# Two attention-and-FFN schedules: the first four tiles' q and k in blocks of four heads, bias products as units of their own, twelve output buffers

## The chip, the cores and the metric

The kernel runs on one core of a Trainium2 chip. The metric is the device time of one execution in microseconds (us). The engines are PE (TensorE, matrix products), DVE (VectorE), ACT (ScalarE), POOL (GpSimd) and SP (SyncE, which here only issues transfers). PE writes its results into PSUM, which has eight banks of 128 x 512 fp32.

## The reference

Attention over q, k, v of shape [4, 8, 768, 64] (batch, heads, positions, head size). A query sees the 95 positions before it and itself, and the first 8 positions of its sequence (the global keys). A linear bias with one slope for each head (ALiBi) is taken off the scores. The result is read as 3072 rows of 512 numbers and goes through a layer with three weights and a maximum:

```python
scores = scale * np.matmul(q, k.transpose(0, 1, 3, 2))
keep = is_global | is_local
dist = np.where(is_global & ~is_local, float(n_local), np.abs(rel))
scores = np.where(keep, scores - slopes * dist, -1e9)
x = softmax(scores) @ v                      # -> [3072, 512]
h = np.maximum(np.maximum(x @ w1, x @ w2), x @ w3)   # w1..w3 [512, 768]
out = h @ w_out                              # w_out [768, 512]
```

(The last lines are the reference put together and shortened.)

## The kernel before

The 3072 rows are cut into 24 tiles T of 128 rows, six for each sequence of the batch. Two tiles form a pair G for loading. The FFN works on seven chunks of 4, 2, 2, 4, 4, 4 and 4 tiles.

All work is written out by hand in one string, SCHEDULE (lines 24 to 86). It is a list of units such as `F0.4.1@3`: a letter for the kind, numbers for what it works on, behind them for most copying units a digit for the engine (0 ACT, 1 DVE, 2 POOL), and behind the @ the buffer. The loop of lines 545 to 552 emits the units in that order; each engine executes its own units in the order of the string, and the framework adds the waits between engines that data and buffers need. SP issues transfers in the same manner, in the order of the string.

The kinds that matter here:

- `l` loads q, k or v (L213 for the first four tiles together, called group 12; L220 else), `c` casts them to bf16 (L185), `v` casts v into the value tile (L238).
- q and k have to be transposed. For the first pairs PE does it: `x` (L252, L258), and `y` copies the result from PSUM into a tile qkT (L266 for the first four tiles, L269). Later pairs use a transposing transfer `X` (L274).
- `G` puts the first 8 keys of a sequence into qkT (L289, L291), `V` puts their values into a value tile (L299 on POOL, L301 on ACT and DVE). `V` of a tile writes over rows that the attention of that same tile still reads, so it follows that tile's `A`.
- `S` are the scores of a tile and a group of four heads. S1.0, for instance, is tile 1, heads 0 to 3. With a last digit of 1, two matmuls first put the bias into PSUM (L313), and the score matmuls add to it (L321); with 0 there are only score matmuls, and the bias is applied after the exponential as a multiplication by a table, `m` (L337 for two blocks, L339 for the first tile of a sequence). `e` is the exponential on ACT (L328).
- `A` multiplies by the values (L363, L366), `n` normalises on DVE (L374, L375). The result is transposed for the FFN by PE (`t`, L390, and the copy `u`, L393) or by a transposing transfer `Z` (L396).
- `F` is one of the three products for one of six blocks of 128 hidden columns: `Fc.f.j@bank`, four matmuls (L405). `f` takes it out of PSUM: j = 0 copies (L419), j = 1 and 2 take the maximum on DVE (L421, L424).
- `O` is the product with w_out for one tile (L429), `o` copies it to an output buffer (L444), `s` stores it (L450). `E` does the last chunk (L453 to L479).
- `w`, `W`, `q`, `Q` load and cast weights. `D` are dummy matmuls (L506); `B` and `K` make the tables of the bias, `R` their common part.

`F`, `O`, `x` and `t` take one of the eight PSUM banks, `S` and `A` two neighbouring ones, named behind the @. A unit that takes a bank waits until the unit that last read the bank is done; so the choice of banks in the string decides which copy a matmul waits for.

Before the change, the tile qkT of the first four tiles has the layout [128, 2 tiles, q or k, 4 head pairs, 128]; a copy `y` of one half of the heads writes four separate pieces of it. Output buffers are six: three in the buffers of the small weight loads (wst0) and three in those of the large ones (wst1).

Of the kernel before, what the change touches and what calls it, by code (L numbers as in the profile page):

```python
# [12 lines left out]
FP32 = mybir.dt.float32  # L13
# [26 lines left out]
    l2.4.2@1 x3.1.2@7 Q1.2 l1.5.2@3 F0.5.2@0 c1.4.2.2@0 F1.0.2@1 v7.1.2 f1.4.1.1 y3.1.2.0 G6.0 c0.4.2.2  # L40
    f1.2.0.0@2 f0.5.2.1 f1.0.2.1@1 F1.2.1@5 f1.2.1.1 Q0.2 S6.0.0@2 e6.0@4 l0.5.2@4 S7.0.0@6 S7.1.0@0
    S6.1.0@4 F0.4.2@2 f0.4.2.1 e7.1@5 F1.5.0@3 F1.1.0@0 m7.1.1 e7.0@6 m7.0.1 F1.3.0@1 F1.5.1@2 x4.1.2@6
    f1.5.0.0@1 F1.2.2@3 m6.0.1 f1.2.2.1 v8.1.2 l1.6.2@5 e6.1@7 m6.1.1 x4.0.2@7 f1.5.1.1 f1.1.0.0@3 F1.1.1@0
    f1.1.1.1 f1.3.0.0@4 y4.1.2.0@0 A7@4 V7.0.2 v9.0.2 G7.0 v9.1.2 F1.3.1@1 n7@0 y4.0.2.0 Q2.0 c1.5.2.0@2
# [5 lines left out]
    V9.1.1 m10.0.1 S10.1.0@0 e10.1@6 V9.0.0 G10.1 O1.1@7 F2.5.1@2 f2.5.1.1 t8@3 F2.4.1@0 O0.0@1 m10.1.1 X11  # L50
    S11.1.0@4 l1.7.2@0 f2.4.0.0@4 o1.1.0@2 e11.1@4 v11.0.0 u8.1@0 S11.0.0@2 v10.0.1 f2.4.1.1 A10@6 V10.0.2
    e11.0@7 V10.1.0 X12@2 o0.0.1@2 n10@0 F2.5.2@0 F2.0.2@1 X13 l2.8.2@0 F2.1.0@4 F2.1.2@5 F2.1.1@2 F2.0.1@3
    m11.1.1 f2.5.2.1@0 Z9 F2.4.2@0 Z10 m11.0.1 f2.1.0.0@1 f2.1.1.1 l2.6.2@1 f2.4.2.1 A11@6 n11@3 O1.0@2
    o1.0.0@1 t11@0 u11.0 F2.3.2@4 l0.7.2@1 f2.1.2.1 f2.0.1.1 f2.0.2.1 f2.3.2.1 F2.2.2@3 l0.8.2@2 v12.0.2
# [531 lines left out]
```

## Time and profile before

| what | us |
|---|---|
| median of three runs (176.34 to 176.47) | 176.45 |
| the profiled execution's own time | 176.6 |
| its span, first to last instruction | 174.7 |
| PE busy | 166.9 |
| DVE busy | 127.7 |
| ACT busy | 102.4 |
| POOL busy | 48.9 |

The span is what the profile shows from the first to the last instruction; 1.9 us of the execution lie around it. A row of the timeline reads: start, duration, engine, line of the kernel, operation, what is written and from what, how many instructions, and in brackets how long the engine had been idle before and what released it. PEld is the weight load of PE, which overlaps the matmuls; its idle time alone doesn't mean that PE stood. In the chain of waits each row is a start, a length and what it consists of.

### The profile page before, as it was taken

The numbers are of one execution on the slowest core, as the hardware profiler recorded it, in microseconds if no ns is written. First come the engines' busy times: TensorE is split into PE (matmuls) and PEld (weight loads), VectorE is DVE, ScalarE is ACT, GpSimd is POOL, SyncE is SP. The second block draws the span as 40 slices with busy tenths as digits, with TensorE's granted clock in tenths as the row PEclk, the third lists the DMA queues.
The fourth block names the chain that finished last, engine by engine and source line by source line (L and its number), as shares of the span: only waits on it lengthen the run. The fifth ranks groups of instructions, "written<-read, shape, count | busy, mean of one in ns | idle before, by whom it ended". The sixth has DMA issues, their size and how long they took to land.

```text
span 174.7 us, 3862 instructions
## 1 busy us (share of the span) xinstructions
PE 166.9 (96%) x1489; PEld 93.5 (54%) x1510; DVE 127.7 (73%) x259; ACT 102.4 (59%) x153; POOL 48.9 (28%) x94
## 2 busy tenths in 40 slices
PE   7799999999999999999999999999999999999992
PEld 2346745576956867644456445554444554444442
DVE  7798969784868988589697287839859993059930
ACT  5979895487995876746257994721375651310022
POOL 4056536349370300196614003200203210000000
PEclk9999999999999999999999999999999999999999
DMA  5999999999999898998989498999992134047106
GB/s 148 352 292 312 363 351 379 294 319 345 270 230 267 193 145 194 290 319 198 232 146 196 119 253 200 290 159 260 272 184 68 32 90 64 0 180 240 60 10 234
DMA packets 66658, 37.35 MB, mean 214 GB/s; under 512 B 24144, under 2 KB 61904, under 8 KB 66640
## 3 DMA queue, kind: packets, MB, share of 16 engines
q1 hardware_dynamic: 66496, 37.04, 84.5%
q8 instruction: 12, 0.20, 0.5%
q10 hardware_dynamic: 144, 0.07, 0.1%
q14 instruction: 6, 0.05, 0.1%
HBM read 25.17 MB, written 6.29 MB: 180 GB/s over the span
## 4 chain that ended last, share of the span: by engine, by line
PE 83%; DVE 5%; DMA 4%; ACT 3%; issue 2%; SPq 1%; ACTq 0%
PE psum L405 50%; PE psum L429 18%; PE psum L321 5%; DMA rawqq<-in_q_dram 4%; PE psum L363 4%; PE psum L366 3%; PE psum L258 2%; DVE qkT L266 1%; ACT P L328 1%; PE psum L390 1%; DVE h L421 1%; DVE P L337 1%; PE psum L313 1%; SPq L213 1%; ACT qb L185 1%
## 5 line engine op out<-in xcount | busy, mean ns | idle before, releaser
L405 PE MATMUL psum<-xT,w 128*128 128x512 bf16 (+1 forms) x491 | 99.3, 348 | 1.1
L405 PEld LDWEIGHTS <-w 128*128 128x128 bf16 x504 | 47.5, 98 | 43.1 <-issue 2.7
L328 ACT ACTIVATE P<-psum 128x1024 bf16<-128x1024 f32 (+1 forms) x48 | 43.3, 953 | 13.5 <-PE psum L321 13.2
L421 DVE TENSOR_TENSOR h<-h,psum 128x512 bf16<-128x512 bf16 (+1 forms) x42 | 24.6, 604 | 16.1 <-PE psum L405 12.6
L429 PE MATMUL psum<-wo,ht 128*128 128x512 bf16 (+2 forms) x148 | 32.9, 362 | 0.6 <-issue 0.3
L337 DVE TENSOR_TENSOR P<-P,wmask 128x1024 bf16<-128x1024 bf16 x35 | 23.8, 695 | 6.2 <-ACT P L328 6.1
L424 DVE TENSOR_TENSOR ht<-h,psum 128x512 bf16<-128x512 bf16 (+1 forms) x42 | 26.1, 643 | 3.0 <-PE psum L405 2.4
L419 ACT CAST h<-psum 128x512 bf16<-128x512 f32 (+1 forms) x32 | 15.6, 517 | 20.1 <-PE psum L405 17.9
L429 PEld LDWEIGHTS <-ht 128*128 128x128 bf16 x156 | 14.0, 98 | 14.1
L238 POOL CAST va<-rawv 64x512 bf16<-64x512 f32 x26 | 16.5, 636 | 13.6 <-DMA rawv<-in_v_dram 12.8
L375 DVE TENSOR_TENSOR xb<-psum,rz 128x512 bf16<-128x512 f32 x24 | 16.6, 691 | 0.8
L299 POOL COPY va<-vaf 4x260 int32<-4x260 int32 x15 | 5.9, 395 | 37.5 <-PE psum L366 37.2
L321 PE MATMUL psum<-qkT 64*128 64x128 bf16 x352 | 14.9, 217 | 1.2 <-DVE qkT L266 0.9
L321 PEld LDWEIGHTS <-qkT 64*128 64x128 bf16 x352 | 10.3, 94 | 9.6 <-issue 6.8
L363 PEld LDWEIGHTS <-P 128*128 128x128 bf16 x192 | 12.3, 97 | 2.4
L363 PE MATMUL psum<-va,P 128*128 128x65 bf16 x160 | 12.5, 193 | 0.1
L444 ACT COPY ost<-psum 128x512 f32<-128x512 f32 x11 | 6.4, 589 | 8.9 <-PE psum L429 8.2
L366 PEld LDWEIGHTS <-P 128*128 128x128 bf16 x160 | 10.4, 97 | 1.5 <-issue 0.3
L434 ACT COPY ost<-psum 128x512 f32<-128x512 f32 (+2 forms) x5 | 2.3, 480 | 15.1 <-PE psum L429 15.0
L366 PE MATMUL psum<-va,P 128*128 128x65 bf16 x128 | 9.9, 193 | 0.0
L301 ACT COPY va<-vaf 4x520 bf16<-4x520 bf16 x10 | 6.2, 620 | 3.8 <-PE psum L366 3.7
L374 DVE RECIPROCAL rz<-psum 128x8 f32<-128x8 f32 x24 | 4.8, 202 | 4.7 <-PE psum L366 3.7
(69 smaller groups left out, 134.4 us busy)
## 6 DMA issues: line engine op xcount, KB each, us to landing
rawv<-in_v_dram SPq DMA_DIRECT2D x12, 512.0 KB, 6.3
rawq<-in_q_dram SPq DMA_DIRECT2D x10, 512.0 KB, 7.3
rawk<-in_k_dram SPq DMA_DIRECT2D x10, 512.0 KB, 7.0
out_dram<-ost SPq DMA_DIRECT2D x19, 256.0 KB, 2.6
wst<-in_moe_w_dram SPq DMA_DIRECT2D x3, 1024.0 KB, 10.9
wst<-in_moe_w_dram SPq DMA_DIRECT2D x3, 512.0 KB, 8.1
wost<-in_moe_w_out_dram SPq DMA_DIRECT2D x3, 512.0 KB, 7.3
out_dram<-ost SPq DMA_DIRECT2D x9, 128.0 KB, 1.8
```

What stands on the lines that cost most here:

```text
L238: copies[how](heads(va(T))[64 * e:64 * e + 64, :, 0:D], src)
L321: nc.tensor.matmul(sp[:, hh, j2, ds], qT(T - ds, 1)[hsl, jp], qT(T, 0)[hsl, jp], start=not how, stop=True, skip_group_check=True)
L328: nc.scalar.activation(P[:, :, 0:n], sps[T, g].rearrange("p a b d n -> p (a b) d n")[:, :, 0:n], AF.Exp, bias=0.0, scale=scale)
L337: mul(P, P, wmask[:, g, :, 0:2])
L363: nc.tensor.matmul(o, P[:, i, 0], heads(va(T))[:, h], start=True, stop=(t == 0), skip_group_check=True)
L366: nc.tensor.matmul(o, P[:, i, 1], heads(va(T - 1))[:, h], start=False, stop=True, skip_group_check=True)
L375: nc.vector.tensor_tensor(out=x.rearrange("p (g h) d -> p g h d", g=2), in0=o4[:, :, :, 0:64], in1=rz[:, :, :, None].to_broadcast([128, 2, ...
L405: nc.tensor.matmul(ps, w123[f // 2][:, j, dm, (f % 2) * 128:(f % 2) * 128 + 128], xT[c][:, dm], start=(dm == 0), stop=(dm == 3))
L419: copies[how](h01, ps)
L421: nc.vector.tensor_max(h01s[c, f], h01s[c, f], ps)
L424: nc.vector.tensor_max(dst, h01s[c, f].rearrange("p (t e i) -> p t e i", e=2, i=64), ps.rearrange("p (t e i) -> p t e i", e=2, i=64))
L429: nc.tensor.matmul(po, ht[c][:, f, tt * 128:(tt + 1) * 128], wo[:, f, cols], start=(f == 0), stop=(f == NF - 1))
```

## The change

1. The tile qkT of the first four tiles gets the layout [128, q or k, half of the heads, 2 tiles, 2 head pairs, 128]. One copy `y` now writes one block that lies together, and the scores of a group of heads read only its own block. `G` is adapted to it.
2. The two bias matmuls become a unit `b` of their own, which takes the banks; `S` with a last digit of 1 adds to them. There are eight such units. The scores S1.1 get the bias too, and the multiplication m1.1.1 is left out. Four dummy units are added, ten matmuls of 256 columns in all.
3. Output buffers are twelve, called os (a new entry of RINGS), laid over the place of wst1 in one tile that holds wst0 as well.
4. SCHEDULE has 781 units in place of 770. Many units move by a few places, get another bank, or another engine. Among the moves: v9, v16 and v17 go from POOL to ACT; u2 from ACT to DVE; u6 from DVE to ACT; v21.0 stands ahead of f4.1.0 on ACT; V4.0 ahead of f0.3.0; the store s0.1 ahead of Z15.

The diff, with the string cut to its first lines and to the places that are spoken of:

```diff
 SCHEDULE = """
...
-    y0.0.1.0@0 w0.2@2 D3.256@1 x12.1.1@1 y0.1.1.1 S0.1.1@2 c1.12.0.1 c0.12.0.1 S1.1.0@4 K1 x12.1.0@6
-    y0.1.0.1 G0.2 y1.0.1.0@1 e1.1@0 m1.1.1 v0.0.2 v1.0.2 e0.1@1 v0.1.2 D3.256@0 x12.0.0@0 y0.0.0.0 S1.0.1@2
-    w1.0@0 G1.0 e1.0@2 y1.1.0.1 S0.0.1@4 e0.0@3 y1.1.1.1 y1.0.0.1 S2.1.1@6 e2.1@4 v1.1.2 S2.0.1@2 G2.2
-    v2.1.1 v2.0.1 A0@0 n0@0 v3.0.2 l2.2.2@2 w1.1@1 A1@4 V1.1.2 e2.0@5 v3.1.2 n1@1 S3.0.1@6 c0.2.2.0@2 V1.0.1
+    x12.1.1@1 y0.0.1.0@0 K6 y0.1.1.1 b0.1@2 c1.12.0.1 b1.1@4 D3.256@6 S1.1.1 c0.12.0.1 S0.1.1 v0.0.2
+    x12.1.0@6 y0.1.0.1 G0.1 w0.0@1 w0.2@2 y1.0.1.0@1 e1.1@0 v0.1.2 D3.256@0 x12.0.0@0 v1.0.2 v1.1.2 e0.1@1
+    y0.0.0.0 b1.0@2 b0.0@4 D2.256@7 S1.0.1 G1.0 e1.0@2 S0.0.1 y1.1.0.1 y1.1.1.1 w1.0@0 b2.1@6 S2.1.1 e0.0@3
+    e2.1@4 y1.0.0.1 b2.0@2 D2.256@0 S2.0.1 v2.1.1 v2.0.1 A0@0 n0@0 G2.2 v3.0.2 l2.2.2@2 A1@4 V1.1.2 b3.1@6
+    n1@1 v3.1.2 b3.0@0 S3.0.1 e2.0@5 w1.1@1 c0.2.2.0@2 e3.0@6 S3.1.1 V1.0.1 t1@2 c1.2.2.1 u1.1@0 w1.2@2 A2@4
...
-    e3.1@7 l1.3.2@6 A3@0 t2@4 l0.3.2@0 y2.0.2.0 W0.1.2 n3@3 t0@3 u2.0 S4.0.0@6 u0.1 e4.0@1 S4.1.0@4 t3@2
+    n2@2 t0@3 V2.1.2 x2.0.2@0 V2.0.2 G3.2 x2.1.2@1 y2.1.2.1@2 e3.1@7 A3@6 n3@3 l0.3.2@6 y2.0.2.0 t2@2 W0.1.2
+    u2.1 l1.3.2@0 S4.0.0@0 e4.0@1 S4.1.0@4 G4.0 u0.1 t3@6 u3.1 D3.256@2 S5.0.0@0 V3.1.0 e5.0@3 W0.0.1 W0.2.2
...
-    V3.0.1 F0.3.0@5 m4.1.1 f0.0.1.1 f0.1.1.1 f0.1.2.1@0 v4.0.0 v4.1.0 F0.2.0@2 f0.3.0.0@2 A4@6 F0.5.0@0
-    V4.0.0 l2.3.2@0 W2.1.1 W1.1.2 q1@0 W1.2.0 F0.4.1@3 l1.4.2@1 f0.0.2.1 n4@1 F0.5.1@4 c1.3.2.2@1 V4.1.1
+    F0.1.0@1 v5.0.2 F0.0.2@0 F0.1.2@2 f0.1.0.0@1 W2.0.1 F0.4.0@3 m4.1.1 F0.3.0@1 f0.0.1.1 l2.3.2@0 F0.2.0@6
+    v4.0.0 f0.1.1.1 v4.1.0 A4@4 V4.0.0 q1@0 f0.3.0.0@2 f0.1.2.1@0 F0.5.0@2 W1.1.0 W2.1.1 W1.2.0 F0.4.1@1
...
-    v11.1.0 V8.0.0 V8.1.2 F2.2.0@3 f2.3.0.0@2 f2.2.0.0@0 f2.5.0.1@1 f1.3.2.1 n8@1 l0.6.2@6 F2.3.1@7 f2.3.1.1
-    F2.2.1@1 f2.2.1.1 F2.4.0@6 c0.6.2.0@1 f2.0.0.0@3 A9@2 n9@2 v10.1.1 c1.6.2.2 X10@1 S10.0.0@4 e10.0@5
+    o0.3.1@0 O0.1@1 S9.0.0@2 o0.2.0@1 Z7@2 u6.0 S9.1.0@4 e9.1@0 F1.1.2@0 F2.0.0@6 f1.1.2.1 l2.5.2@2 e9.0@3
+    m9.1.1 o0.1.1@2 F2.5.0@7 v11.1.0 F2.3.0@0 F1.3.2@4 m9.0.1 A8@2 n8@1 V8.0.0 l0.6.2@6 V8.1.2 f2.3.0.0@3
+    F2.3.1@1 f1.3.2.1 F2.2.0@5 f2.5.0.0@0 F2.4.0@0 f2.0.0.1@1 G9.0 f2.2.0.0@2 F2.2.1@7 A9@2 V9.1.2 f2.2.1.1
...
-    S17.1.0@6 v19.0.0 V15.0.0 e17.1@1 e17.0@3 V15.1.0 O2.0@5 F4.4.0@6 m16.0.1 v19.1.0 s0.1 s3.2 s0.3 s1.0
+    v18.1.2 c0.9.2.0 V15.1.0 G16.0 Z14 e16.0@0 o3.2.1@7 V15.0.0 e16.1@2 s0.1 O3.0@3 n15@3 m16.0.1 O3.3@0 Z15
...
-    n17@2 A18@2 n18@0 G18.1 F4.5.2@7 F4.1.0@6 l0.10.2@1 v21.1.0 c0.10.2.0@0 f4.1.0.0@3 A19@0 F4.0.1@2
-    F4.1.1@3 n19@3 F4.3.2@6 l1.11.2@0 Z16@2 Z17 Z18 Z19 F4.0.0@0 c1.10.2.2 f4.1.1.1 f4.0.0.1@4 c1.11.2.1@2
-    f4.2.2.1 F4.0.2@1 F4.5.1@0 f4.5.1.1 v20.0.1 F5.4.0@3 l0.11.2@3 l2.11.2@2 V19.0.2 v20.1.1 f4.5.2.1 s2.1
+    n18@2 F4.1.0@5 F4.5.0@6 f4.5.0.0@1 A19@2 c0.10.2.0@0 v21.1.0 v21.0.0 f4.1.0.0@4 G18.2 n19@3 F4.0.1@7
+    F4.1.1@6 Z16@2 s1.0 Z17 Z18 F4.0.0@2 f4.1.1.1 f4.0.0.1@3 F4.5.1@3 f4.5.1.1 f4.2.2.1 V19.0.1 F4.0.2@5
+    F4.3.2@2 Z19 F5.4.0@1 c1.11.2.0@2 F5.2.1@3 v20.1.1 f4.3.2.1 c1.10.2.0 l0.11.2@2 l2.11.2@2 F5.2.0@2
...
-LAST_BANKS = (7, 6, 4, 5, 2, 0, 3, 1)
-LAST_STAGES = ((2, 1, 0), (2, 0, 1))
+LAST_BANKS = (6, 3, 7, 2, 0, 5, 1, 4)
+LAST_STAGES = (3, 1, 11, 6, 10, 8, 7, 2, 5, 4, 9, 0)
...
+    staging = persist.tile([128, 2048 * RINGS["wst1"] + 1024 * RINGS["wst0"]], FP32, name="staging")
+    staged = {"wst1": (0, 2048), "os": (0, 512), "wst0": (2048 * RINGS["wst1"], 1024)}
...
-            qkT[G] = ring("qkT", slot, [128, 2, 2, NP, 128], BF16, "qkT")
+            shape = [128, 2, 2, 2, NP // 2, 128] if G < 2 and QUAD_USED else [128, 2, 2, NP, 128]
+            qkT[G] = ring("qkT", slot, shape, BF16, "qkT")
...
-            copies[how](dst.rearrange("c t j (e i f) -> c t (j e) i f", e=2, f=2),
+            copies[how](qkT[G][:, a, p].rearrange("c t j (e i f) -> c t (j e) i f", e=2, f=2),
                         src.rearrange("c j e f (t i) -> c t (j e) i f", t=2))
...
+    def u_b(slot, T, g):
+        n = 2 if T % NT else 1
         sp = ring("sp", slot, [128, 2, 2, 2, 128], FP32, "sp")
         sps[T, g] = sp
+        for hh in range(2):
+            nc.tensor.matmul(sp[:, hh, :, 0:n], identb, bias[:, g, hh, :, 0:2] if n == 2 else bias[:, g, hh, :, 2:3],
+                             start=True, stop=False, skip_group_check=True)
...
-        osts[c, tt] = ring(("wst0", "wst1")[chunks[c][tt] % 2], slot, [128, DM], FP32, "ost")
+        osts[c, tt] = ring("os", slot, [128, DM], FP32, "ost")
```

More of the change, by code (lines that the diff above doesn't have):

```diff
@@ L40 @@
[L40 to L44, printed above, removed]
@@ L50 @@
[L50 to L54, printed above, removed]
@@ L181, in cast @@
     def cast(how, dst, src):
-        n = src.shape[1]
-        for lo, hi in (((0, n // 2), (n // 2, n)) if how == 2 else ((0, n),)):
-            copies[how](dst[:, lo:hi], src[:, lo:hi])
+        if how != 2:
+            copies[how](dst, src)
+            return
+        first = src.shape[1] > 1
+        n = src.shape[1 if first else 2] // 2
+        for half in (slice(0, n), slice(n, 2 * n)):
+            s = (slice(None), half) if first else (slice(None), slice(None), half)
+            copies[how](dst[s], src[s])
     def words(ap):
```

135 lines of the change are left out of this document (76 added, 59 removed).

## The prediction

> **What bounds the kernel now.** I read the page's busy shares first, then the kinds of its chain of waits, then the busy times by stage, then the waits of PE.
>
> ```profile
> span 174.7 us, 3862 instructions
> ...
> PE 166.9 (96%) x1489; PEld 93.5 (54%) x1510; DVE 127.7 (73%) x259; ACT 102.4 (59%) x153; POOL 48.9 (28%) x94
> ...
> PE 83%; DVE 5%; DMA 4%; ACT 3%; issue 2%; SPq 1%; ACTq 0%
> ```
> ```profile
> 0.00:13.10 13.10, 10.45 (x80) 4.96 (x80) 10.37 (x34) 10.05 (x20) 3.99 (x13) 1.00 0.94 264
> 13.10:21.50 8.40, 8.23 (x158) 5.80 (x158) 7.38 (x17) 7.78 (x10) 4.90 (x12) 1.00 1.12 335
> 21.50:166.20 144.70, 142.88 (x1221) 79.74 (x1238) 108.22 (x206) 82.24 (x120) 40.02 (x70) 1.00 0.86 207
> 166.20:174.70 8.50, 5.30 (x36) 2.98 (x35) 1.71 (x3) 2.30 (x5) 0.00 (x0) 1.00 0.36 125
> ```
>
> The columns of the second view are the stretch, its length, and the busy times of PE, weight loads, DVE, ACT and POOL. PE is the bound: 96% of the span. I cut the span where the FFN's first matmuls start (21.5) and where the last chunk's W_out work starts (166.2). In the middle PE is busy for 142.88 of 144.70 us, so 1.82 us is an upper bound for what freed waits can give back there, but nothing limits what a new wait adds: a stall of PE in the middle goes into the time at its full length. Before 21.5 the first tiles' loads, copies and exponentials set the pace; there ACT is busy for 7.78 of 8.40 us.
>
> **The change part by part.** I replayed the new string against the old one engine by engine: for each PE unit, which unit on another engine it has to follow, and when that one would end if durations stay.
>
> *Start: block layout, bias units, m1.1.1 gone.*
>
> ```profile
> 10.69 0.60 DVE P L337
> 11.29 1.80 DVE qkT L266 x3
> ```
> ```profile
> 12.31 0.60 PE L313 MATMUL psum<-bias,identb 128*128 128x512 bf16 x2
> 13.14 0.40 PE L321 MATMUL psum<-qkT 64*128 64x128 bf16 x8 [0.22 <-DVE qkT L266]
> 15.04 0.69 DVE L375 TENSOR_TENSOR xb<-psum,rz 128x512 bf16<-128x512 f32 x1
> 19.50 0.58 ACT L393 COPY xT<-psum 128x512 bf16<-128x512 bf16 x1 [0.31 <-PE psum L390]
> 20.80 0.79 PE L321 MATMUL psum<-qkT 64*128 64x128 bf16 x16
> ```
> ```profile
> 11.95 3.57 ACT L328 ACTIVATE P<-psum 128x1024 bf16<-128x1024 f32 x4
> ...
> 16.34 1.04 ACT L328 ACTIVATE P<-psum 128x1024 bf16<-128x1024 f32 x1
> ```
>
> The score matmuls of tile 2 waited until 13.14 for the last of three q, k copies, 0.22 us of it idle, though they read another half's data: S2.1 reads heads 4 to 7, the last copy writes heads 0 to 3. The block layout takes that false wait away, and without the mask multiplication (0.60 us in the chain) the copies come up to 0.6 earlier. But ACT runs its four exponentials without a pause from 11.95 to 15.52, so the scores come earlier to an engine that is still busy: I take 0 to −0.2 for this. Next late is S3.0: its bias unit now lies on the banks of A0 and follows n0, which ends at 15.73; two bias matmuls (half of 0.60 each, overlapped, about 0.45) and the scores (about 0.33 to the last start) bring its exponential to 16.5 instead of 16.34, +0.15. The copy u2 goes from ACT, where it stood 0.58 us directly ahead of e4.0, to DVE: e4.0 may start up to 0.3 earlier, but the 16 score matmuls of tile 5 that end at 21.59 still stand ahead of F0.0.1 and wait for banks. The two further bias matmuls (about 0.22 each, by their spacing) and the ten matmuls of 256 columns in four new dummy units (about 0.11 each) lie where PE waits for ACT and DVE; without that cover they would cost about 1.5. Start: −0.05, with ends −1.26 (the whole multiplication, taken at 0.68, and all of u2, 0.58, on the path) and +0.5 (S3.0 late, a fifth of the added matmuls uncovered, nothing gained).
>
> *f0.3.0.0 goes behind V4.0.0 on ACT.*
>
> ```profile
> 28.64 0.59 ACT L419 CAST h<-psum 128x512 bf16<-128x512 f32 x1 [0.74 <-PE psum L405]
> 29.79 2.75 PE L405 MATMUL psum<-xT,w 128*128 128x512 bf16 x11
> 30.01 0.62 ACT L301 COPY va<-vaf 4x520 bf16<-4x520 bf16 x1 [0.78 <-PE psum L366]
> ```
> ```profile
> 114.18 9.09 PE L405 MATMUL psum<-xT,w 128*128 128x512 bf16 x40
> ```
>
> Before, the evacuation f0.3.0.0 ran at 28.64, ahead of V4.0.0, which writes the global rows into tile 4's values and has to wait until A4 has read them. Now V4.0.0 is first, so f0.3.0.0 waits for A4 as well, and F0.4.1 newly takes the bank that it empties, with only F0.5.0 between. A 512-column matmul is 9.09 less one length of 0.38, over 40, 0.22 us, a unit of four 0.87. In the times of before: F0.5.0 covers 29.79 to 30.66; V4.0.0 ends at 30.63, f0.3.0.0 at about 31.2. PE waits 31.2 − 30.66 = +0.55 (ends 0.4 and 0.7, by how far ACT overlaps two instructions).
>
> The Trainium skill (Perfetto Trace Analysis, section Tensor Engine Instruction) says that ACT, DVE and GpSimd take their instructions strictly in order while PE can pull weight loads ahead of running matmuls. These rows agree: V4.0.0 idles for 0.78 us for A4 although it is at its engine's head. By that rule nothing can slip past V4.0.0; were it otherwise, this term would be 0.
>
> *f2.3.0.0 behind V8.0.0.*
>
> ```profile
> 57.79 0.62 ACT L301 COPY va<-vaf 4x520 bf16<-4x520 bf16 x1 [0.46 <-PE psum L366]
> 58.32 0.62 ACT L419 CAST h<-psum 128x256 bf16<-128x256 f32 x2
> ```
> ```profile
> 57.57 1.97 PE L405 MATMUL psum<-xT,w 128*128 128x256 bf16 x16
> ```
>
> The order on ACT stays, but F2.4.0 now takes the bank of F2.3.0 (before, a bank long free), and only F2.3.1 and F2.2.0 stand between A8 and it. At 0.11 per 256-column matmul (1.97 less 0.19, over 16) they cover 57.57 to 58.45; the two evacuations take 0.62 together, the first of them ends at about 58.7 and its release is seen a little later: +0.3 (0.2 to 0.4).
>
> *v21.0.0 ahead of f4.1.0.0.*
>
> ```profile
> 111.91 0.58 ACT L419 CAST h<-psum 128x512 bf16<-128x512 f32 x1 [1.10 <-PE psum L405]
> 112.52 0.62 ACT L238 CAST va<-rawv 64x512 bf16<-64x512 f32 x1
> 113.16 1.04 ACT L185 CAST qb<-rawq 128x1024 bf16<-128x1024 f32 x1
> ```
> ```profile
> 119.04 0.72 DVE L424 TENSOR_TENSOR ht<-h,psum 128x512 bf16<-128x512 bf16 x1
> ```
>
> F5.4.0 now takes the bank that f4.2.2.1 empties, fourth on DVE from f4.1.1.1, which follows f4.1.0.0. On ACT, from f4.5.0.0's start: 0.58 + 0.62 + 0.62 (the added cast) + 1.04 + 0.58 = 3.4; on DVE four maxima and copies of at most 0.72, which overlap by some 0.07: 2.6; in all 6.0. PE's cover after F4.5.0 is A19 (16 short matmuls, estimated at 0.5) and six units of 0.87, 5.7. +0.25 (0 to 0.5).
>
> *u6 to ACT.*
>
> ```profile
> L328 ACT ACTIVATE P<-psum 128x1024 bf16<-128x1024 f32 x40 | 39.3, 1022 | 11.9 <-PE psum L321 11.5
> ```
>
> u6 stood on DVE; now it is behind e8.1, v9.1.0, e8.0, v9.0.0, c1.5.2.0 and o0.2.0, and F1.1.2 takes the bank that it empties: 2 × 1.02 + 2 × 0.62 + 1.04 + 2 × 0.58 = 5.5 from the end of S8.1. PE's cover is S8.0, S9.0, S9.1 (0.40 at most, like S2.1's eight matmuls, so about 1.1), t6 (four short ones, estimated at 0.2) and 18 W_out matmuls at 0.22: 5.2. +0.15 (0 to 0.4). The cast c1.5.2.0, and with it the transposing transfer X10, comes later by the two exponentials and two casts, some 3 us at most; I take this as hidden, and price it among the rivals.
>
> *Waits removed.* Four places where PE stood:
>
> ```profile
> 66.34 1.01 ACT L328 ACTIVATE P<-psum 128x1024 bf16<-128x1024 f32 x1
> ...
> 67.40 0.42 PEld L405 LDWEIGHTS <-w 128*128 128x128 bf16 x4 [0.29 <-issue]
> ```
> ```profile
> 132.33 1.28 DVE L421 TENSOR_TENSOR h<-h,psum 128x512 bf16<-128x512 bf16 x2
> ...
> 133.07 0.53 PEld L405 LDWEIGHTS <-w 128*128 128x128 bf16 x3 [0.35 <-issue]
> ```
> ```profile
> 60.76 0.59 PE L429 MATMUL psum<-wo,ht 128*128 128x512 bf16 x2 [0.16 <-issue]
> ```
> ```profile
> 99.42 1.24 PE L429 MATMUL psum<-wo,ht 128*128 128x512 bf16 x5 [0.16 <-issue]
> ```
>
> F2.1.1 stood behind e11.0's bank until 67.35: 0.29; F5.5.2 behind f5.1.1.1 until 133.0: about 0.2 of the 0.35, since weight loads run ahead; the two W_out units 0.16 each. The new banks take all four away: −0.8 (ends −0.3, if the units that now take those banks wait in turn, and −1.82, all that the middle has).
>
> *Staging.* Twelve output buffers instead of six, same copies, same stores. Nothing in PE's waits comes from a store, so 0. The cover is that a buffer comes round again only after several stores; with twice as many buffers it gets larger. The remaining moves (stores ahead of Z15, casts between POOL, ACT and DVE) I put at 0: behind them lies PE's queue of FFN units. The tail keeps its instructions and lengths: 0.
>
> Sum: −0.05 + 0.55 + 0.3 + 0.25 + 0.15 − 0.8 = +0.4. The profiled execution took 176.6 us (span 174.7 and 1.9 around it), so 177.0; it stands 0.15 above the median of the runs, so on the median 176.85.
>
> **Rivals.** *Faster by the start.* If ACT's queue is what sets 13.1 to 21.5 (7.78 busy of 8.40), taking u2 off it and giving it work sooner pays in full: −1.26 in place of −0.05. The sum is then 1.25 − 0.8 − 1.26 = −0.8, 175.65. It decides from a start of −0.8 on. Against it: the exponentials themselves don't become fewer, and n0 now stands ahead of S3.0.
>
> *No change.* The new waits are half as long because PE comes later to them (each stall gives the next release time): +0.65 − 0.05 − 0.8 = −0.2, 176.25; or the freed waits and new ones cancel, 176.45.
>
> *Slower still: a transpose lands late.*
>
> ```profile
> 100.79 0.59 PE L405 MATMUL psum<-xT,w 128*128 128x512 bf16 x2
> ```
> ```profile
> 96.57 1.19 SPq L396 DMA_TRANSPOSE xT<-xb  x1
> ```
> ```profile
> xT<-xb SPq DMA_TRANSPOSE x1, 4.1
> ```
>
> The last two rows are Z15, the last transpose of the fifth chunk: issued at 96.57, landed 4.1 later at 100.67, and F4.4.0, its first reader, starts at 100.79, with no margin. The new order puts a store ahead of Z15 in SP's queue. If that store delays it by as much as one issue takes here, up to 1.19, less the 0.12 of margin, half of it on PE after other units, about 0.5, and X10's readers wait 0.3, then +0.4 becomes +1.2: 177.65.
>
> *The false wait stays.* If the dependency is kept over the whole tile whatever its layout, S2.1 gains nothing and S3.0 is late: +0.3 instead of −0.05, 177.2.
>
> *Faster by the engines' sharing.*
>
> ```profile
> 76.45 1.09 DVE L337 TENSOR_TENSOR P<-P,wmask 128x1024 bf16<-128x1024 bf16 x1
> ...
> 78.88 0.68 DVE L337 TENSOR_TENSOR P<-P,wmask 128x1024 bf16<-128x1024 bf16 x1
> ```
> ```profile
> 76.32 1.70 POOL L185 CAST qb<-rawq 128x512 bf16<-128x512 f32 x2
> ```
>
> A mask multiplication took 1.09 here, beside a POOL cast, and 0.68 two microseconds later, without one. Several casts of that stretch leave POOL for ACT. Two such meetings fewer (0.41 each) on releases that PE waits for are −0.8: 176.05. Against it: at 76 PE ran FFN units without a pause.
>
> The Trainium skill (SBUF — State Buffer, section Who interferes with whom) states a lock: a DVE instruction with two SBUF inputs and a GpSimd one that reads SBUF contend. The 1.09 agrees with that in kind; no row here shows which of the two was held up, or for how long.
>
> **How the numbers follow.** A measurement of this kernel tells about 0.2%, 0.35 us, from no change. Forecast 0.45; late transpose 0.10; false wait 0.05: slower 0.60. No change 0.16. Faster by the start 0.18, by sharing 0.06: 0.24. The forecast's own range, all four new waits at their ends, is 176.3 to 177.7. The whole range goes from 175.8, leaving out the best starts, to 177.8, leaving out two late transposes together: about 2 in 10.
>
> **What would show it.** Right: a gap on PE of about 0.5 after F0.5.0 with line 419 on ACT behind line 301; one of 0.3 among the 256-column units at 58; no idle at 67.4 and 133; the first FFN matmul within 0.3 of 21.5; PE's busy time as before and the middle longer by about 0.4. Wrong: the first FFN matmul before 20.8, or a middle no longer than 144.3, or a transpose named as what PE waited for.

## The result and the profile after

The changed kernel took 178.06 us (median of six, 177.67 to 178.31) against 176.46 for the kernel before: a ratio of 1.0083, 95% interval 1.0065 to 1.0102. It is slower by 1.6 us where 0.4 was forecast, and lies outside the range. The profiled execution took 178.12 us, its span is 176.0, 1.3 more than before.

The code moved by some lines: what was L301 is now L325 (global value rows), L363 and L366 are L391 and L394 (attention times v), L393 is L421 (`u`), L405 is L433 (`F`), L419, L421 and L424 are L447, L449 and L452 (`f`), L337 and L339 are L365 and L367 (`m`). First the busy shares and the kinds of the chain of waits, from the page of the changed kernel:

```profile
span 176.0 us, 3889 instructions
...
PE 169.5 (96%) x1522; PEld 95.1 (54%) x1522; DVE 126.5 (72%) x256; ACT 108.3 (62%) x163; POOL 44.2 (25%) x85
...
PE 76%; ACT 9%; DVE 6%; DMA 4%; issue 3%; SPq 1%; ACTq 0%; DVEq 0%
```

PE is busy for 96% as before, so this view says nothing of the loss (the profile of before also lacked 21 of its matmul records, which shows as idle time where PE had none; this comes back below). The chain does: ACT has 9% of it where it had 3%. The waits of PE say where:

```profile
PE psum L433 <- ACT xT L421: 0.4, 1, 0.4
PE psum L433 <- DVE rz L402: 0.3, 1, 0.3
PE psum L418 <- DVE xb L403: 0.2, 1, 0.2
PE psum L433 <- DVE h L449: 0.2, 1, 0.2
PE psum L433 <- DVE ht L452: 0.2, 1, 0.2
```

FFN matmuls (L433) now stand for copies, four times; before, this view named no FFN matmul at all. The second row names DVE's reciprocal as the releaser; that is the last instruction by the profile, not the cause, as the next fence shows. The timeline of the changed kernel at four places, ACT or DVE ahead of the matmul that waited:

```profile
30.24 0.62 ACT L325 COPY va<-vaf 4x520 bf16<-4x520 bf16 x1 [2.35 <-PE psum L394]
30.77 0.57 ACT L447 CAST h<-psum 128x512 bf16<-128x512 f32 x1
...
31.39 0.59 PE L433 MATMUL psum<-xT,w 128*128 128x512 bf16 x2 [0.35 <-DVE rz L402]
```
```profile
50.87 1.02 ACT L356 ACTIVATE P<-psum 128x1024 bf16<-128x1024 f32 x1 [0.80 <-PE psum L349]
51.91 0.62 ACT L254 CAST va<-rawv 64x512 bf16<-64x512 f32 x1
52.56 1.02 ACT L356 ACTIVATE P<-psum 128x1024 bf16<-128x1024 f32 x1
53.48 0.61 ACT L254 CAST va<-rawv 64x512 bf16<-64x512 f32 x1
54.11 1.04 ACT L195 CAST qb<-rawk 128x1024 bf16<-128x1024 f32 x1
55.06 0.58 ACT L471 COPY staging<-psum 128x512 f32<-128x512 f32 x1
55.53 0.59 ACT L421 COPY xT<-psum 128x512 bf16<-128x512 bf16 x1
...
56.17 0.92 PE L433 MATMUL psum<-xT,w 128*128 128x256 bf16 x7 [0.36 <-ACT xT L421]
```
```profile
59.06 0.62 ACT L325 COPY va<-vaf 4x520 bf16<-4x520 bf16 x1 [0.46 <-PE psum L394]
59.59 0.62 ACT L447 CAST h<-psum 128x256 bf16<-128x256 f32 x2
60.00 0.27 PE L433 MATMUL psum<-xT,w 128*128 128x256 bf16 x1
```
```profile
116.87 1.26 ACT L254 CAST va<-rawv 64x512 bf16<-64x512 f32 x2
118.04 0.57 ACT L447 CAST h<-psum 128x512 bf16<-128x512 f32 x1
118.64 0.69 DVE L449 TENSOR_TENSOR h<-h,psum 128x512 bf16<-128x512 bf16 x1 [2.03 <-ACT h L447]
...
120.44 0.72 DVE L452 TENSOR_TENSOR ht<-h,psum 128x512 bf16<-128x512 bf16 x1
...
121.22 1.02 PE L433 MATMUL psum<-xT,w 128*128 128x512 bf16 x4 [0.21 <-DVE ht L452]
```

Each shows the same thing: a copy that empties a bank stands in its queue behind work that was put ahead of it, and the matmul starts right when the copy ends (31.34, 56.12, the first of two at about 59.9, 121.16). An idle time in brackets counts from the end of the matmul before, which overlaps the next; the time that PE loses is the spacing of the starts beyond the usual 0.216 us for 512 columns (the median in this trace).

To see how much PE is late at each place, although the two kernels do their units in different order, I took each unit's start less the nominal length of all PE work that its string puts ahead of it, and compared the two kernels, with the plain difference at the first FFN matmul as the start:

| place in the changed kernel | PE later than before, us | step there |
|---|---|---|
| first FFN matmul (21.74, before 21.52) | 0.21 | start |
| after F0.4.1 (31.39) | 0.74 | +0.51, f0.3.0.0 |
| after F1.4.2 (48.77) | 1.0 | +0.2 to 0.3 in this execution, not foreseen |
| F1.1.2 (56.17) | 1.28 | +0.40, u6 |
| after F2.4.0 (60.00) | 1.50 | +0.23, f2.3.0.0 |
| after F2.1.1 | 1.27 | −0.28, wait removed |
| F4.1.0 (113.27) | 1.29 | nothing |
| F5.4.2, past F4.3.2 and F5.4.0 | 1.86 | +0.57, v21.0.0 |
| F5.3.2, past F5.5.2 | 1.73 | −0.2, wait removed |
| last chunk's W_out (167.63, before 166.18) | 1.45 | −0.3, small gaps of the last FFN chunk |

The rows come from one execution of each kernel, and some waits move from one execution to the next: F1.4.2 starts at 48.23 in the kernel before, at 48.49 in b_stage12, which has the same string, and at 48.05 in b_order, which changes one unit far ahead of it (both below). A step of 0.2 or 0.3 that no experiment bears out can be of this kind.

### The profile page after: what moved, and what is told of

Read it like the earlier page. It is cut to its first block, busy times and chain, and to the rows that moved or that the text cites. A ratio compares the mean times of both kernels' runs of the same rounds, so it can differ in the third digit from the quotient of the medians.

```text
span 176.0 us, 3889 instructions
## 1 busy us (share of the span) xinstructions
PE 169.5 (96%) x1522; PEld 95.1 (54%) x1522; DVE 126.5 (72%) x256; ACT 108.3 (62%) x163; POOL 44.2 (25%) x85
## 4 chain that ended last, share of the span: by engine, by line
PE 76%; ACT 9%; DVE 6%; DMA 4%; issue 3%; SPq 1%; ACTq 0%; DVEq 0%
PE psum L433 49%; PE psum L457 14%; PE psum L349 5%; DMA rawqq<-in_q_dram 4%; ACT P L356 4%; PE psum L391 3%; PE psum L394 2%; DVE h L449 1%; ACT va L254 1%; ACT qb L195 1%; PE psum L335 1%; SPq L229 1%; DVE xb L403 1%; DVE P L365 1%; DVE h L447 1%
## 5 line engine op out<-in xcount | busy, mean ns | idle before, releaser
L433 PE MATMUL psum<-xT,w 128*128 128x512 bf16 (+1 forms) x504 | 100.1, 348 | 1.3 <-ACT xT L421 0.4
L433 PEld LDWEIGHTS <-w 128*128 128x128 bf16 x504 | 47.7, 98 | 43.9 <-issue 3.9
L457 PE MATMUL psum<-wo,ht 128*128 128x512 bf16 (+2 forms) x156 | 33.6, 363 | 0.0
L449 DVE TENSOR_TENSOR h<-h,psum 128x512 bf16<-128x512 bf16 (+1 forms) x42 | 24.8, 605 | 11.8 <-PE psum L433 8.4
L452 DVE TENSOR_TENSOR ht<-h,psum 128x512 bf16<-128x512 bf16 (+1 forms) x42 | 26.0, 642 | 4.8 <-PE psum L433 4.2
L365 DVE TENSOR_TENSOR P<-P,wmask 128x1024 bf16<-128x1024 bf16 x34 | 23.9, 714 | 6.5 <-ACT P L356 6.3
L447 ACT CAST h<-psum 128x512 bf16<-128x512 f32 (+1 forms) x30 | 14.8, 507 | 17.4 <-PE psum L433 10.5
L403 DVE TENSOR_TENSOR xb<-psum,rz 128x512 bf16<-128x512 f32 x24 | 16.6, 692 | 0.8
L254 POOL CAST va<-rawv 64x512 bf16<-64x512 f32 x20 | 12.9, 644 | 11.6 <-DMA rawv<-in_v_dram 10.7
L323 POOL COPY va<-vaf 4x260 int32<-4x260 int32 x16 | 6.4, 398 | 32.7 <-PE psum L394 30.2
L349 PE MATMUL psum<-qkT 64*128 64x128 bf16 x352 | 14.1, 217 | 0.4 <-DVE h L449 0.2
L391 PEld LDWEIGHTS <-P 128*128 128x128 bf16 x192 | 12.4, 97 | 2.2
L391 PE MATMUL psum<-va,P 128*128 128x65 bf16 x160 | 12.4, 193 | 0.0
L325 ACT COPY va<-vaf 4x520 bf16<-4x520 bf16 x12 | 7.4, 619 | 6.3 <-PE psum L394 6.2
L394 PEld LDWEIGHTS <-P 128*128 128x128 bf16 x160 | 10.4, 97 | 1.4 <-issue 0.2
L471 ACT COPY staging<-psum 128x512 f32<-128x512 f32 x10 | 5.9, 586 | 7.1 <-DVE staging L471 6.4
L447 DVE CAST h<-psum 128x512 bf16<-128x512 f32 (+1 forms) x12 | 7.8, 661 | 3.0 <-PE psum L433 3.0
L394 PE MATMUL psum<-va,P 128*128 128x65 bf16 x128 | 9.9, 193 | 0.0
L254 POOL CAST vaf<-rawv 64x512 bf16<-64x512 f32 x8 | 5.8, 722 | 13.2 <-DMA rawv<-in_v_dram 12.9
```

Source lines behind the costliest of these rows:

```text
L254: copies[how](heads(va(T))[64 * e:64 * e + 64, :, 0:D], src)
L349: nc.tensor.matmul(sp[:, hh, j2, ds], qT(T - ds, 1, hsl, jp), qT(T, 0, hsl, jp), start=not how, stop=True, skip_group_check=True)
L365: mul(P, P, wmask[:, g, :, 0:2])
L391: nc.tensor.matmul(o, P[:, i, 0], heads(va(T))[:, h], start=True, stop=(t == 0), skip_group_check=True)
L394: nc.tensor.matmul(o, P[:, i, 1], heads(va(T - 1))[:, h], start=False, stop=True, skip_group_check=True)
L403: nc.vector.tensor_tensor(out=x.rearrange("p (g h) d -> p g h d", g=2), in0=o4[:, :, :, 0:64], in1=rz[:, :, :, None].to_broadcast([128, 2, ...
```

## The experiments

### Taking the new waits out, one at a time

Theory: each place where PE newly stands goes into the time at full length, and they add. Rival: a wait that is taken away comes back later, or the loss has another cause. Each of these kernels is the changed one with one unit moved. The ratios compare with runs of the kernel before that stood beside each; its median lay between 176.46 and 176.59, so differences between times of two sections are uncertain by about 0.1.

```diff
-v4.1.0 A4@4 V4.0.0 q1@0 f0.3.0.0@2 f0.1.2.1@0
+v4.1.0 f0.3.0.0@2 A4@4 V4.0.0 q1@0 f0.1.2.1@0
```


> The changed kernel with one unit moved back: f0.3.0.0 ahead of A4 and V4.0.0 on ACT. The trace of the changed kernel shows PE standing 0.52 us ahead of F0.4.1. Theory (stalls add up): that wait goes, PE reaches F0.4.1 with no gap, and the time falls by 0.5, from 178.06 to about 177.55. Rival (the wait is given back later, because the FFN units behind it wait for copies and loads that do not come earlier): the gap at F0.4.1 goes, but gaps of together about 0.5 appear before the sixth tile's scores, and the time falls by less than 0.2.

Measured: 177.63 (177.35 to 178.06), 1.0064 times the kernel before (1.0046 to 1.0081); 0.43 less than the changed kernel. The gap of 0.52 ahead of F0.4.1 is gone from the trace, and PE is about 0.47 earlier from there to the last chunk (167.15 there in place of 167.63).

```diff
-u6.0
+u6.1
```


> The changed kernel with the copy u6 on DVE again, at the same place of the string. PE stands 0.36 to 0.55 us ahead of F1.1.2 in the changed kernel. Theory: minus 0.4, about 177.65. Rival (DVE, which then has masks and maxima in front of u6, is as late as ACT, or the exponential e9.1 that comes earlier does not matter): less than 0.2 faster.

Measured: 177.55 (177.33 to 178.13), ratio 1.0063 (1.0046 to 1.0080), 0.5 less. The gap ahead of F1.1.2 is gone from the trace. In the one profiled execution, though, PE reached the last chunk at 167.64, no earlier than in the changed kernel: there PE stood 0.41 us ahead of F1.1.1, earlier in the same chunk, where it stood 0.1 in the changed kernel. That wait has nothing to do with u6; it belongs to the part on POOL and DVE below.

```diff
-v21.1.0 v21.0.0 f4.1.0.0@4
+v21.1.0 f4.1.0.0@4 v21.0.0
```


> The changed kernel with v21.0.0 put behind f4.1.0.0 on ACT. The changed kernel shows PE standing 0.20 ahead of F4.3.2 and 0.37 ahead of F5.4.0. Theory: the chain ACT to DVE gets shorter by one cast, 0.62, both waits go, minus 0.55, about 177.5. Rival: f4.1.1.1 was not held by v21.0.0 but by DVE's own queue, then less than 0.2 faster.

Measured: 177.82 (177.31 to 178.08), ratio 1.0070 (1.0053 to 1.0086), 0.24 less, under half of the 0.55 that was expected. Both gaps at 120 and 121 are gone; PE gains 0.5 between F4.1.0 and F5.4.2. The profiled execution had lost 0.4 of it ahead of that place, most at F3.5.1 (80.46, a gap of 0.47).

```diff
-F2.3.0@0 F1.3.2@4 m9.0.1 A8@2 n8@1 V8.0.0 l0.6.2@6 V8.1.2 f2.3.0.0@3
+F2.3.0@0 F1.3.2@4 m9.0.1 f2.3.0.0@3 A8@2 n8@1 V8.0.0 l0.6.2@6 V8.1.2
```

For this one the changed kernel ran again on the same chip, as a_again:

> The changed kernel itself, with the string only broken into other lines, as a base on this chip. 178.0, 1.5 above the kernel before.

> The changed kernel with f2.3.0.0 ahead of A8 and V8.0.0. The changed kernel shows PE standing 0.29 ahead of F2.4.0. Theory: that gap goes, 0.3 shorter than the changed kernel. Rival (F2.4.0 then waits for another evacuation on ACT, or A9 for its exponentials): less than 0.1 shorter.

Measured: a_again 178.23 (178.19 to 178.24), ratio 1.0101 (1.0085 to 1.0117); a_f23 178.11 (177.66 to 178.31), ratio 1.0090 (1.0076 to 1.0104). The gap ahead of F2.4.0 is gone, and PE gains 0.3 from F1.1.2 (56.02 against 55.96) to F2.4.0 (59.56 against 59.79). In the time it is 0.1 where 0.3 was expected, within the intervals: too little for this measurement.

### All four together

> The changed kernel with four units moved: f0.3.0.0 ahead of V4.0.0, u6 on DVE, f2.3.0.0 ahead of V8.0.0, v21.0.0 behind f4.1.0.0. Theory (stalls of PE add up one for one): 0.52 + 0.4 + 0.29 + 0.55 = minus 1.75, about 176.3, so no slower than the kernel before. Rival (given back later, or another cause behind the loss, the start or the port): at least 177.2.

Measured: 176.59 (176.13 to 177.31), ratio 1.0002 (0.9989 to 1.0015). Of the 1.6 us, 1.47 are gone, and the kernel stands level with the one before. The trace shows none of the four gaps; the last chunk's W_out starts at 165.75, 1.88 earlier than in the changed kernel. The waits of PE in it, from the answer on waits:

```profile
PE psum L268 <- DVE qbq L193: 1.3, 2, 0.7
PE psum L530 <- DVE cap L548: 1.2, 1, 1.2
PE psum L416 <- DVE xb L401: 0.2, 1, 0.2
PE psum L347 <- DVE h L447: 0.2, 1, 0.2
PE psum L455 <- issue: 0.2, 1, 0.2
```

No FFN matmul (here L431) is named any more. The theory that stalls of PE add up fits: in the trace the gaps of 0.52, 0.40, 0.29 and 0.57 are 1.78, and PE is 1.88 earlier; in the times 0.43 + 0.5 + 0.24 + 0.1 are 1.3 from the single kernels, 1.47 together. Taken singly, each kernel's interval overlaps that of the changed kernel, so one by one it is the traces that show the waits; the four together are clear of the noise (at most 1.0015 against at least 1.0065).

### One new wait alone, in the kernel before

```diff
-F0.2.0@2 f0.3.0.0@2 A4@6 F0.5.0@0 V4.0.0
+F0.2.0@2 A4@6 F0.5.0@0 V4.0.0 f0.3.0.0@2
```


> The kernel before with f0.3.0.0 put behind V4.0.0 on ACT, banks unchanged. Theory (the order alone costs nothing; it is the bank that makes PE wait for the late copy): F0.4.1 has another bank and starts without a gap, 176.5, no change. Rival (a late evacuation costs by itself, since the maxima behind it on DVE come late and free their banks late): +0.3 to +0.5.

Measured: 176.55, ratio 0.9994 (0.9983 to 1.0005). No change, with the evacuation as late as in the changed kernel: here are ACT and PE of this run, where `F` is L403.

```profile
30.02 0.62 ACT L299 COPY va<-vaf 4x520 bf16<-4x520 bf16 x1 [2.25 <-PE psum L364]
30.55 0.57 ACT L417 CAST h<-psum 128x512 bf16<-128x512 f32 x1
```
```profile
30.23 1.67 PE L403 MATMUL psum<-xT,w 128*128 128x512 bf16 x7
```

The copy ends at 31.12, and PE runs through. Then the bank is changed as well:

```diff
-F0.4.1@3
+F0.4.1@5
```


> The kernel before with f0.3.0.0 behind V4.0.0 on ACT, and F0.4.1 on the bank that f0.3.0.0 empties: this one part of the change alone. Theory: PE stands 0.5 ahead of F0.4.1 and the time is 0.5 longer, about 177.0. Rival (the kernel before has slack further on that takes the stall up): less than 0.2 longer.

Measured: 177.04, ratio 1.0022 (1.0010 to 1.0034). In this kernel t4 writes over the bank of F0.4.1 before that unit was read, so that block 4 of the first chunk isn't computed as in the reference; the next one moves t4.

> The kernel before with f0.3.0.0 behind V4.0.0 on ACT, F0.4.1 on the bank that f0.3.0.0 empties, and the transpose t4 on bank 3, which F0.4.1 had. Theory: PE stands 0.5 ahead of F0.4.1, the time is 0.5 longer than before, about 177.0. Rival (slack further on takes the stall up): less than 0.2 longer.

Measured: 176.86 (176.5 to 177.38), ratio 1.0017 (1.0001 to 1.0032), 0.3 to 0.4 longer (by the ratio or by the medians). PE stands 0.52 at the place:

```profile
30.06 0.59 PE L403 MATMUL psum<-xT,w 128*128 128x512 bf16 x2
31.01 0.38 PE L403 MATMUL psum<-xT,w 128*128 128x512 bf16 x1 [0.35 <-DVE rz L372]
```

So neither the order nor the bank costs by itself: b_order has the late copy and the old bank, a_v4 has the new bank and the early copy, and neither trace has the gap. The bank turns a late copy into a wait of PE. That the time grows by less than the 0.52 leaves room for the rival's slack further on; which part it took up isn't shown.

### The start: layout and dummies

a_oldlayout keeps order, bias units and dummies, and gives the first four tiles the old layout (the line below, and the lines of `y`, `G` and `S` that write and read the tile).

```diff
-            shape = [128, 2, 2, 2, NP // 2, 128] if G < 2 and QUAD_USED else [128, 2, 2, NP, 128]
+            shape = [128, 2, 2, NP, 128]
```


> The changed kernel with the old layout of the first four tiles' q and k; order, bias units and dummies stay. Theory (ACT's exponentials set the pace, the false wait cost little): the scores of tile 2 start about 0.15 later, after the third of the three copies, the exponential e2.1 not more than 0.1 later, and the time stays within 0.2 of 178.0. Rival (the block layout is what keeps the new start as fast as the old): at least 0.4 slower than the changed kernel.

Measured: 178.35 (178.32 to 178.96), ratio 1.0107 (1.0086 to 1.0129), 0.3 more than the changed kernel, with intervals that overlap. The expectation had the mechanism wrong. In the new order the scores S2.1 stand ahead of the copy y1.0.0, so they don't wait for it; with the old layout it is the copy that waits until the scores have read the tile. DVE's rows of the two kernels (L283 is the copy), first a_oldlayout, then the changed kernel:

```profile
13.07 0.69 DVE L283 COPY qkT<-psum 128x512 bf16<-128x512 bf16 x1 [1.00 <-ACT P L354]
```
```profile
11.44 1.28 DVE L283 COPY qkT<-psum 128x512 bf16<-128x512 bf16 x2
```

The first row names an exponential as the releaser only because that ended at 13.05; in the changed kernel the same copy runs while that exponential does. What the old layout adds is a wait for PE, whose last matmul of S2.1 ends at 12.96. With blocks the copies end at 12.72, with the old layout at 13.76; the scores S2.0 start at 13.87 and 14.13, the first FFN matmul at 21.74 and 22.00. In the new order the layout is worth 0.26 at the start, by one execution of each.

> The changed kernel without the four dummy units that were added (six plus four matmuls on zeros). Theory: they stand where PE waits anyway, so 0, the first FFN matmul at the same 21.7. Rival (they delay tile 5's scores and tile 1's): the first FFN matmul 0.1 to 0.3 earlier. Other rival (without them PE gets slower at the start): the first transposes and scores longer, the first FFN matmul later than 22.

Measured: 177.76 (177.72 to 177.91), ratio 1.0067 (1.0052 to 1.0083), 0.3 less than the changed kernel, with intervals that overlap. The first FFN matmul starts at 21.26 in place of 21.74: 0.48, more than even the rival had; 0.05 of it stand ahead of the place of these dummies already (x12.0.0 starts at 10.13 in place of 10.18). PE's timeline at S2.0, changed kernel first:

```profile
13.13 0.59 PE L335 MATMUL psum<-bias,identb 128*128 128x512 bf16 x2
13.56 0.38 PE L532 MATMUL psum<-zeros 128*128 128x256 bf16 x2
13.87 0.40 PE L349 MATMUL psum<-qkT 64*128 64x128 bf16 x8
```
```profile
12.94 0.59 PE L332 MATMUL psum<-bias,identb 128*128 128x512 bf16 x2
13.46 0.40 PE L346 MATMUL psum<-qkT 64*128 64x128 bf16 x8
```

The scores follow the bias matmuls at once when there is no dummy between: 0.52 in place of 0.74 after the bias unit's start. The third theory, that PE needs the dummies, falls: the scores of eight matmuls take 0.40 in both. Of the 0.48, 0.27 are left at the last chunk. Which of the dummies it is was asked on top of a_all4:

> a_all4 without the two added dummy units of two matmuls (ahead of the scores S1.0 and S2.0), with the two of three matmuls kept. Theory: it is these two that stand in PE's way, so nearly all of the 0.48 at the first FFN matmul is gained. Rival (the three ahead of S5.0 are the ones): the first FFN matmul less than 0.2 earlier.

> a_all4 without the four added dummy units. Theory: the first FFN matmul 0.48 earlier, as in a_nodummy, of which at least 0.3 is left at the end: 0.3 to 0.5 faster than the kernel before. Rival (a floor by the fifth chunk's transposes takes it up): as a_all4, level with the kernel before.

Measured: the first FFN matmul at 21.25 without the two units of two matmuls, at 21.18 without all four, against 21.74 with them: the two units of two are nearly all of it. Ahead of S2.0 PE had nothing to wait for. Ahead of S1.0 it had a little: in a_nodummy the last bias matmul starts at 11.12 and S1.0 at 11.42, when the copy y0.0.0 has ended (11.36); with the dummy it starts at 11.61. In the times a_all4nd took 176.11 (175.74 to 176.53), ratio 0.9981 (0.9969 to 0.9993); a_all4d2 took 176.41 (175.65 to 177.38), ratio 1.0001 (0.9984 to 1.0019), too wide to confirm the gain that its trace shows.

### POOL and DVE

> The changed kernel with the cast Q0 on POOL put behind the two casts v8.1 and v8.0. In the changed kernel the half-size mask multiplication m6.0.1 takes 0.83 us while Q0 runs on POOL, and m7.0.1 and m6.1.1 0.76 and 0.83; f1.5.1.1 behind them comes late, and PE stands 0.37 ahead of F1.4.2. Theory (POOL and DVE hold each other up): with the shorter POOL casts there the multiplications take 0.42 and 0.68 where no POOL cast has started ahead of them, the gap at F1.4.2 gets smaller, the time 0.2 to 0.35 shorter. Rival (the multiplications' time has nothing to do with POOL): lengths and gap as before, no change.

```diff
-e6.1@7 m6.1.1 v8.0.2 l1.6.2@5
+e6.1@7 m6.1.1 v8.0.2 Q0.2 l1.6.2@5
```
(and Q0.2 taken from its place ahead of l0.5.2)

The timeline of DVE and POOL, changed kernel first:

```profile
45.80 0.83 DVE L367 TENSOR_TENSOR P<-P,wmask 128x512 bf16<-128x512 bf16 x1
...
46.88 0.76 DVE L365 TENSOR_TENSOR P<-P,wmask 128x1024 bf16<-128x1024 bf16 x1
47.56 0.82 DVE L367 TENSOR_TENSOR P<-P,wmask 128x512 bf16<-128x512 bf16 x1
48.31 0.74 DVE L449 TENSOR_TENSOR h<-h,psum 128x256 bf16<-128x256 bf16 x2
```
```profile
45.59 1.51 POOL L201 CAST wo<-staging 128x512 bf16<-128x512 f32 x2 [1.58 <-DMA staging<-in_moe_w_out_dram]
47.16 1.70 POOL L254 CAST va<-rawv 64x512 bf16<-64x512 f32 x2
```

Then a_q0late, where the multiplications are L363 and L365 and the cast of w_out is L199:

```profile
45.81 0.82 DVE L365 TENSOR_TENSOR P<-P,wmask 128x512 bf16<-128x512 bf16 x1
...
46.89 0.68 DVE L363 TENSOR_TENSOR P<-P,wmask 128x1024 bf16<-128x1024 bf16 x1
47.49 0.42 DVE L365 TENSOR_TENSOR P<-P,wmask 128x512 bf16<-128x512 bf16 x1
```
```profile
44.73 1.63 POOL L199 CAST wo<-staging 128x512 bf16<-128x512 f32 x2 [0.73 <-DMA staging<-in_moe_w_out_dram]
```

POOL's cast ends at 46.36. Ahead of that the half-size multiplication takes 0.82, after it 0.42; the full one 0.68 in place of 0.76. F1.4.2, whose bank the maximum behind them empties, starts at 48.40 in place of 48.77 with no gap. So the multiplications are long beside a POOL cast and short without one. That the edit took PE's gap away isn't shown: in a_again, the changed kernel without it, POOL's casts ended at 47.25, m6.1.1 behind them took 0.41, and F1.4.2 started at 48.55 with no gap either. The time, 177.99 (177.78 to 179.16), ratio 1.0095 (1.0060 to 1.0130), is too wide to show 0.3.

The Trainium skill (SBUF — State Buffer, section Who interferes with whom) says that a DVE instruction with two SBUF inputs and a POOL one that reads SBUF exclude each other, and that whichever starts first holds the other up. The rows agree on both halves. Above, casts that had started first lengthened the multiplications. In a_all4 a multiplication was running when the cast of w_out started at 45.29, and m6.0.1 followed it at once: they kept 0.68 and 0.42, and the cast took 1.97, against 1.17 in a_again, where hardly any of it met one (44.21 to 45.38).

```profile
44.70 0.68 DVE L363 TENSOR_TENSOR P<-P,wmask 128x1024 bf16<-128x1024 bf16 x1
45.29 0.42 DVE L365 TENSOR_TENSOR P<-P,wmask 128x512 bf16<-128x512 bf16 x1
```
```profile
45.29 1.97 POOL L199 CAST wo<-staging 128x512 bf16<-128x512 f32 x2 [1.59 <-DMA staging<-in_moe_w_out_dram]
```

The gaps at F1.1.1 in a_u6 and at F1.4.2 in the changed kernel come from the same stretch, with m7.1.1 at 0.98 in a_u6 and 0.67 in the changed kernel; they differ between two profiled executions of the changed kernel too (F1.1.1 at 47.03 and F1.4.2 at 48.77, in a_again 47.19 and 48.55). The kernel before has such a gap too, 0.19 ahead of F1.4.2 in its profiled execution, 0.33 in b_stage12 and none in b_order, so that the change added to it isn't shown. Which of the two engines comes first there seems to hang on when a load lands (POOL's row above names the DMA as its releaser); that the landing decides was not tried.

### Staging alone, and a faster kernel

> The kernel before with the twelve output buffers laid over the place of the large weight loads, taken in turn; nothing else changed. Theory (no wait of PE came from a store): 0, within 0.2 of the kernel before. Rival (shared space makes copies wait for weight casts or stores): copies of line 444 wait, +0.2 or more.

Measured: 176.65, ratio 1.0003 (0.9984 to 1.0022). Twelve buffers change nothing that these runs can tell, about 0.2%.

> The changed kernel with the four waits taken out as in a_all4, without the four added dummy units, and with f1.5.1.1 ahead of m6.1.1 on DVE. Theory (the parts add): a_all4 stood level with the kernel before, the dummies cost 0.3 of what is left, the maximum 0 to 0.2: 0.3 to 0.5 faster than before, about 176.2. Rival (the transfers set a floor there: the last transpose of the fifth chunk lands no earlier): not faster than the kernel before by more than 0.1, with PE standing ahead of F4.4.0.

Measured: 175.77 (175.65 to 176.32), ratio 0.9956 (0.9941 to 0.9971). It beats both kernels: 0.7 us faster than the kernel before, more than the 0.3 to 0.5 that were expected, and 2.3 faster than the changed one. The rival had a floor at the fifth chunk's transposes: F4.4.0 starts at 100.66, as in a_all4 (100.65), but in a_all4nd at 100.12, so there is none. Whether the moved maximum has a part is open: a_all4nd without it took 176.11, their intervals just touch, and the profiled execution of a_best was its slowest (176.32).

## Why the prediction was wrong

The direction was right, and so was what makes it: copies pushed back in ACT's queue, with a bank that needs them soon. The size was not. Four terms were mis-sized, together by 1.1 of the 1.2 us that the forecast lacks: u6 by 0.25, v21 by 0.3, the waits removed by 0.3 and the start by 0.26.

**f0.3.0.0 behind V4.0.0, +0.55**: right. 0.52 in the trace, 0.43 in the time of a_v4 (0.3 to 0.4 in b_order_bank2). The chain was as worked out, to 0.1 us. That order alone is free was not said and is shown by b_order.

**f2.3.0.0 behind V8.0.0, +0.3**: right in the trace, 0.29, of which 0.23 are new, since the kernel before stood 0.07 close by (F2.2.1). The time alone doesn't show it.

**v21.0.0, +0.25, and u6, +0.15**: the mechanism right, both terms mis-sized: 0.57 and 0.40. The chains had the lengths that were forecast: 6.0 forecast and 5.97 from 115.19 to 121.16; 5.5 forecast and 5.25 from 50.87 to 56.12. What failed is the step that set a chain on the copying engine against "PE's cover after F4.5.0" as if both began together. PE starts its next unit (A19 at 114.99) 0.2 before the evacuation of the unit that it just left can start (115.19), and likewise S8.0 at 50.66 and e8.1 at 50.87. That 0.2 belongs to each chain that begins behind PE. With it, u6 ends 5.46 after S8.0 began (56.12), and F1.1.2 starts 0.05 later; PE's units between take 5.1: 0.4. For v21 the same sum is 6.17 and 0.06 against 5.66: 0.57. Besides, the prediction's own figures for u6, 5.5 against 5.2, give 0.3 or a little less where it put 0.15. On the way to F5.4.0 PE also stood 0.2 ahead of F4.3.2, for the bank of f4.0.0.1, which the step did not list; this lies inside the 0.57 and adds nothing to it, since F5.4.0 could not start before 121.16 either way.

**Waits removed, −0.8**: about −0.5. F2.1.1 gave 0.28 and F5.5.2 about 0.2, as forecast. The two W_out units, 0.16 each in the sum, had no wait to give back: what failed there is the reading of the rows at 60.76 and 99.42. A unit `O` has six matmuls, and the prediction's row at 99.42 shows five for O2.0; the view of before shows five for O1.1 at 60.76 too. b_stage12 has the same string and all its records, and there O1.1 has six matmuls and starts at 60.79, 0.15 after the last score matmul (60.64), with no idle time:

```profile
60.28 0.57 PE L330 MATMUL psum<-qkT 64*128 64x128 bf16 x14
60.79 1.47 PE L438 MATMUL psum<-wo,ht 128*128 128x512 bf16 x6
```

O2.0 starts there at 99.44 in the same way. An idle time with no releaser named was the place of a matmul that the profile had lost.

**The start, −0.05**: +0.21, inside the ends that were given. The step that failed is "lie where PE waits for ACT and DVE", which put the added dummies at nothing: two of the four units stand between a bias unit and its scores, one where nothing was being waited for and one where the wait was shorter than they are, and the four cost 0.43 to 0.48 (a_nodummy). All the rest of the start then gives about −0.25, by difference. a_oldlayout puts the blocks at 0.26 in the new order, so the rest, without m1.1.1 and with the bias units and u2 moved, comes to about nothing; this was not measured by itself.

Two forecasts of the start came true for another reason. e2.1 gains 0.11 (13.46 against 13.57), within 0 to 0.2, but the blocks didn't take the false wait away: the new order did, which has S2.1 ahead of the copy y1.0.0. S2.1 starts at 12.59 with blocks and 12.56 with the old layout, against 13.14 before, and e2.1 at 13.42 with the old layout. The blocks serve the copy and S2.0. And e3.0 stands at 16.62, forecast 16.5, before 16.34; b3.0 does wait for n0 (it starts at 15.65, n0 ends at 15.60), but without the dummies e3.0 starts at 16.21, so that it is later than before at all is the dummies' doing, and the size agrees by luck.

**Faster by the engines' sharing**: this rival was looked at in the wrong place and with one sign only. The runs show multiplications lengthened by POOL's casts ahead of F1.4.2, where PE loses 0.2 to 0.3 more than before in the two profiles that the table compares. But a_again has no gap there and b_stage12 one of 0.33, so neither sign is shown as an effect of the change.

Of the others: the late transposes did not come, F4.4.0 follows its unit of W_out without a gap. The kernel before did stand there, 0.3 by the spacing of its starts (100.28 to 100.79), a wait that the prediction saw only as a lack of margin; the changed kernel has more small gaps on the way from F3.0.0 to F4.4.0 instead (0.44 in all, against 0.18), so that the two nearly cancel. The false wait is gone; staging is 0 as forecast. The prediction's own range, from the ends of its four new waits, comes to 176.2 to 177.6; it says 176.3 to 177.7. Put together from measured terms, start 0.21, new waits 0.52 + 0.23 + 0.57 + 0.40, F1.4.2 0.25, removed −0.5, and the small gaps of the last FFN chunk −0.3 (0.15, 0.08 and 0.13 before, 0.08 in the changed kernel) come to 1.4 of the 1.45 by which PE is late at the last chunk.

## What to carry to other kernels

Where PE is busy all the time, look at each bank that is used again: list the copy that empties it, all that now stands ahead of that copy on its engine, and PE's units between. A late copy costs nothing until a bank needs it, and from there on most of the stall goes into the time (0.43 of 0.52 in a_v4, 0.3 to 0.4 of 0.52 in b_order_bank2). Start such a chain at the moment the copying engine can see the result, not when PE goes on to its next unit. Before an idle time without a releaser is booked as a wait, count the matmuls of the unit behind it. Dummy matmuls are work like any other: put between two dependent units that follow each other without a wait, they cost what they take.
